# Attention with a feed-forward gate: part of the VectorE pair shifts given to GpSimd

## The chip, the cores and the metric

One core of a Trainium2 chip runs the program. It has five engines with a queue of instructions each: TensorE (PE in the profile, with its weight loads as PEld), ScalarE (ACT), VectorE (DVE), GpSimd (POOL) and SyncE (SP), which here issues DMAs. The metric is the time of one execution on the device, in microseconds (us).

## The reference

Multi-query attention over 2048 tokens with 32 heads of width 16, one K and one V for all heads, plus a gated feed-forward block on the same normalised input; the result is `x + attention * silu(ffn)`.

```python
xn = layernorm(x)                                   # 2048 x 512, bf16
q = (xn @ wq).reshape(B, S, 32, 16)                 # wq 512 x 512
k, v = xn @ wk, xn @ wv                             # 2048 x 16 each
p = softmax(einsum("bhqd,bkd->bhqk", q, k) * 16 ** -0.5)
s = einsum("bhqk,bkd->bhqd", p, v).reshape(B, S, 512) @ wo
f = (silu(xn @ w_gate) * (xn @ w_up)) @ w_down      # inner width 1792
out = x + s * silu(f)
```

## The kernel before

The scores of 32 heads x 2048 queries x 2048 keys are cut into 1024 tiles of 128 keys x 1024 columns (two heads x 512 queries). 32 blocks `b` (four chunks of 512 queries, four groups of eight heads, two halves) have 32 tiles each: 16 key tiles `t` for `x` = 0 and `x` = 1, the two pairs of heads of the block. Two matmuls of 32 rows each make a tile (`sc_emit`, L890) in one of three PSUM slots `ring[0..2]`. The tiles of `x` = 0 and `x` = 1 use different rows of the array, so the four matmuls of two tiles can run together.

A tile is exponentiated in one of two ways. Slots 0 and 1 belong to ScalarE: one exponential of 128x1024 from PSUM into one of `NPB` = 8 buffers `Pb` (`act_sc`, L950). Two such tiles, one of each `x`, are multiplied with `VA` in one group of four column-tiled matmuls (L760). Slot 2 belongs to VectorE (`dve_sc`): "passA" (L1004) turns the scores into 16-bit integers whose bits are a coarse power of two as fp16. Two passes, one of each `x`, fill one buffer `U` of 2048 columns; then for each of two constants `SHIFT[i]` an integer add of the whole buffer (the shift, `dS`, L1020) writes another buffer. The three buffers are multiplied with `VD[:, 0..2]`, which hold V times three coefficients, so that the sum of the three approximates the exponential: three groups of matmuls for a pair (L760). There are ten such buffers (six `Bf` and four quarters of `x_sb`).

All products of a block add up in the one PSUM bank `o_ps`, which VectorE copies out (`oev`, L773) before the next block's products. The sums of the softmax pass through small DMAs and a reciprocal, and GpSimd multiplies (`onorm`, L745). Beside this TensorE computes in the bank `m_ps` the q projections, the feed-forward block (gate and up, each evacuated by VectorE, L665 and L670; tanh on ScalarE, L666; product on GpSimd, L673; down projection, L686 and L688) and the output projection (L703, add on GpSimd, L708), each in groups of four column-tiled matmuls (`cmm`, L491).

No engine's order is left to the framework. A planner (`_Sched`) simulates the five engines at build time with a duration for each operation and a latency for each producer (`LAT`), and `chain` fixes each engine's order as planned. `pe_pick` chooses TensorE's next work: a score tile for ScalarE when a slot is free, other ready work if it ends within `TOL` of the time when that score could start, or, where TensorE would be idle for long enough, a group with zero weights (`zero`, `mzero`) if the recent activity is under `ACTMIN`. `pe_do` puts a VectorE tile into the same event as a ScalarE tile when slot 2 comes free within `MERGE`. Changing between score mode (row tiles) and the rest (column tiles) is planned at `SWITCH`. A block's last `D_LIM` = 12 tiles are not given to VectorE, which goes on with the next block. In the planner, shifts on VectorE and any operation on GpSimd exclude each other (`LOCKS`). The number of tiles that go to VectorE is not written anywhere: it comes out of this plan.

Of the kernel before, what the change touches and what calls it, by code (L numbers as in the profile page):

```python
# [14 lines left out]
ALU = mybir.AluOpType  # L15
# [13 lines left out]
SHIFT = (0.0, 683.0, 341.0)  # L29
# [3 lines left out]
NWARM, NJUNK = 13, 200  # L33
D_START, D_LIM, D_LIM_END = 26, 12, 8
F_ON, F_OFF = 26, 60
PB_URG, AHEAD, LAZY, ACTMIN, ACTLOW = 6, 16, 8, 9.0, 0.8
DPRI, DTOL, DWIN = -1.0, 0.12, 0.15
TOL, MERGE = 0.17, 0.25


def _dims(A_x, A_wq, B_w_gate):
# [143 lines left out]
class _Sched:  # L185
    LAT = {"PE": 0.205, "ACT": 0.22, "DVE": 0.25, "POOL": 0.16, "DMA": 0.0, "EXT": 0.0}
    SAME = {"PE": 0.0, "ACT": 0.0, "DVE": 0.1, "POOL": 0.05, "DMA": 0.0}
    SWITCH = 0.105
    HOT = 0.3
    LOCKS = ("dS", "xn")  # L190

# [94 lines left out]
def kernel(  # L286
# [13 lines left out]
    nc = tc.nc  # L300
# [37 lines left out]
                                        op0=ALU.mult, op1=ALU.add)  # L338
# [34 lines left out]
    xn = [sb([P, D], BF16, f"xn{i}") for i in range(4)]  # L373
    res = xn
    QB = [sb([P, 512], BF16, f"QB{i}") for i in range(2)]
    NPB = 8
    Pb = [sb([P, 1024], BF16, f"Pb{i}") for i in range(NPB)]
    XB = [g2_sb[:, 2 * i:2 * i + 2, :].rearrange("p n d -> p (n d)") for i in range(NT // 2)]
    Bf = [sb([P, 2048], U16, f"Bf{i}")[:] for i in range(6)]
# [117 lines left out]
    def OP(eng, dur, deps, emit, prio, mode=None, name=""):  # L497
        return sd.new(_Op(eng, dur, deps, emit, prio, mode, name))
# [3 lines left out]
        o.start = o.end = t  # L502
        return o

    MMF = 0.215
    NBLK = NSC * NQ * 2
    LN = 4 * (NSC - 1)
    NTILE = NBLK * NT * 2
# [144 lines left out]
    def hT_use(sc, f):  # L653
        return [hT_rd[0][1]] if hT_rd[0] is not None and hT_rd[0][0] == sc - 1 else []
    hT_last = [None]

    def g_ffn(sc, f):
        i = cnt["f"] % 2
        cnt["f"] += 1

        def mm(w, kc):
            return lambda: cmm(m_ps, w[:, kc, f * P:(f + 1) * P], xnT[:, kc, sc * 512:(sc + 1) * 512],
                               kc == 0, kc == KC - 1)
        a = grp_pe([mm(wg_sb, kc) for kc in range(KC)], [ffn_in])
        s_ = OP("DVE", 0.6, [a, ab_rel[i]], lambda: nc.vector.tensor_copy(out=ab[i][:], in_=m_ps[:]), (1,), name="gev")  # L665
        t_ = OP("ACT", 0.477, [s_, th_rel[i]], lambda: nc.scalar.activation(out=th[i][:], in_=ab[i][:], func=ACT.Tanh,  # L666
                                                                            scale=0.5), (0,), name="tanh")
        m_rel[:] = [s_]
        b = grp_pe([mm(wu_sb, kc) for kc in range(KC)], [ffn_in2])
        u_ = OP("DVE", 0.6, [t_, b], lambda: nc.vector.scalar_tensor_tensor(  # L670
            out=th[i][:], in0=th[i][:], scalar=1.0, in1=m_ps[:], op0=ALU.add, op1=ALU.mult), (1,), name="umul")
        m_rel[:] = [u_]
        h = OP("POOL", 1.25, [u_, s_] + hT_use(sc, f), lambda: nc.gpsimd.tensor_tensor(  # L673
            out=hT[:, f, :], in0=ab[i][:], in1=th[i][:], op=ALU.mult), (0,), name="hmul")
        ab_rel[i] = th_rel[i] = h
        h_done[f] = h
# [137 lines left out]
    def rem(b, x):  # L814
        r = NT - nx[b][x]
        if cur["pair"] is not None and cur["pair"][0] == b and cur["pair"][1] == 1 - x:
            r -= 1
        return r
# [162 lines left out]
    def get_buf():  # L981
# [9 lines left out]
        buf_rel[i] = [None]  # L991
        return i, rel

    def dve_sc(si, b, x, start, dur):
        sc, t = place_sc(si, b, x, start, dur)
        first = cur["pair"] is None
        u = cur["np"]
        if first:
            cur["ub"] = get_buf()
        ui, urel = cur["ub"]  # L1000
        U = Bf[ui]
        hs = slice(x * 1024, (x + 1) * 1024)
        pa = OP("DVE", 1.135, [sc] + urel,
                lambda: nc.vector.tensor_scalar(out=U[:, hs], in0=ring[si][:], scalar1=ubias,  # L1004
                                                scalar2=UINF, op0=ALU.add, op1=ALU.min), (1.5, u), name="passA")
        slot[si] = pa
        cur["pa"] = pa
        if first:
            cur["pair"] = (b, x, t, pa)
            return  # L1010
        _, x0, t0, pa0 = cur["pair"]
        cur["pair"] = None
        cur["np"] += 1
        pair_blk.append(b)
        half = b % 2
        tx = {x0: t0, x: t}
        terms, rd = [(ui, [pa, pa0], 0)], []
        for i in range(1, NPH):
            wi, wrel = get_buf()
            o = OP("DVE", 0.6, [pa, pa0] + wrel, lambda wi=wi, i=i: nc.vector.tensor_scalar(  # L1020
                out=Bf[wi], in0=U, scalar1=SHIFT[i], scalar2=None, op0=ALU.add), (2, u, i), name="dS")
            rd.append(o)
            terms.append((wi, [o], i))
        for bi, ops, vi in terms:
            mms = []
            dps = list(ops) + [oev[b - 1]]
            bufv = Bf[bi].bitcast(FP16)
            for g in range(4):
                tt = tx[g // 2]
                mms += mm_of(VD[:, vi], lambda g, bufv=bufv: bufv[:, g * 512:(g + 1) * 512], tt, half, (g,))  # L1030
                dps.append(v_ready[tt // 4][vi + 1])
            pv = OP("PE", MMF, dps, pv_emit(b, mms), (1, b, cur["nA"]), "c", "dpv")
            buf_rel[bi] = [pv] + (rd if vi == 0 else [])
            blk_pv[b].append(pv)
        check_done(b)
# [374 lines left out]
```

## Time and profile before

| | |
|---|---|
| median of 3 runs | 746.0 us (745.09 to 746.49) |
| the profiled execution | 744.99 us, its span from the first to the last instruction 743.1 us |
| TensorE busy | 721.5 us (97%), 8999 matmuls |
| ScalarE busy | 718.1 us (97%) |
| VectorE busy | 682.4 us (92%) |
| GpSimd busy | 127.0 us (17%) |
| granted TensorE clock, mean | 0.996 |
| DMA | 20.68 MB, mean 28 GB/s |

An engine's busy time counts instructions in flight; on ScalarE, VectorE and TensorE an instruction begins before the end of the one ahead of it, so the mean length of one is more than its share of the engine's time. The times of before that the working below rests on are those of the profiled execution.

### The profile page before, as it was taken

The numbers are of one execution on the slowest core, as the hardware profiler recorded it, in microseconds if no ns is written. First come the engines' busy times: TensorE is split into PE (matmuls) and PEld (weight loads), VectorE is DVE, ScalarE is ACT, GpSimd is POOL, SyncE is SP. The second block draws the span as 40 slices with busy tenths as digits, with TensorE's granted clock in tenths as the row PEclk, the third lists the DMA queues.
The fourth block names the chain that finished last, engine by engine and source line by source line (L and its number), as shares of the span: only waits on it lengthen the run. The fifth ranks groups of instructions, "written<-read, shape, count | busy, mean of one in ns | idle before, by whom it ended". The sixth has DMA issues, their size and how long they took to land.

```text
span 743.1 us, 20569 instructions
## 1 busy us (share of the span) xinstructions
PE 721.5 (97%) x8999; PEld 217.0 (29%) x8999; DVE 682.4 (92%) x886; ACT 718.1 (97%) x822; POOL 127.0 (17%) x120
## 2 busy tenths in 40 slices
PE   8999999999999999999999999999999999999994
PEld 3332222222222222222222322222222322322231
DVE  7779999999999899999999999999989999999995
ACT  5999999999999999999999999999999999999992
POOL 3212222200022222200013121220003222220001
PEclk9999999999999999999999999999999999999998
DMA  9400000000011100000001000000001000000001
GB/s 326 151 24 3 23 3 23 2 11 17 3 30 38 38 3 8 18 2 24 3 25 45 21 19 3 25 2 9 17 2 31 24 23 3 6 20 2 24 30 34
DMA packets 21722, 20.68 MB, mean 28 GB/s; under 512 B 8760, under 2 KB 17720, under 8 KB 21624
## 3 DMA queue, kind: packets, MB, share of 16 engines
q1 hardware_dynamic: 20040, 18.73, 8.3%
q8 instruction: 72, 1.18, 0.7%
q10 hardware_dynamic: 1584, 0.56, 0.3%
q14 instruction: 26, 0.21, 0.1%
HBM read 14.71 MB, written 2.34 MB: 23 GB/s over the span
## 4 chain that ended last, share of the span: by engine, by line
ACT 59%; PE 34%; DVE 4%; issue 2%; POOL 0%; ACTq 0%; DVEq 0%; POOLq 0%
ACT Pb L950 54%; PE ring L890 12%; PE o_ps L760 12%; PE m_ps L491 9%; ACT th L666 3%; ACT g_sb L950 1%; DVE Bf L1020 1%; DVE Bf L1004 1%; ACT th L686 1%; DVE x_sb L1020 1%; DVE x_sb L1004 1%; PE ring L491 0%; DVE ab L665 0%; PE ring L455 0%; DVE xn L708 0%
## 5 line engine op out<-in xcount | busy, mean ns | idle before, releaser
L950 ACT ACTIVATE Pb<-ring 128x1024 bf16<-128x1024 f32 x728 | 687.9, 1181 | 3.8 <-PE ring L890 1.9
L890 PE MATMUL ring<-QB,KT 32*128 32x512 bf16 x2048 | 291.7, 383 | 7.1 <-ACT Pb L950 3.9
L1004 DVE TENSOR_SCALAR Bf<-ring 128x1024 uint16<-128x1024 f32 x172 | 209.7, 1219 | 10.9 <-PE ring L890 9.2
L890 PEld LDWEIGHTS <-KT 32*128 32x128 bf16 x2048 | 84.9, 91 | 301.2 <-issue 297.1
L1004 DVE TENSOR_SCALAR x_sb<-ring 128x1024 uint16<-128x1024 f32 x116 | 141.5, 1220 | 7.6 <-PE ring L890 5.8
L760 PE MATMUL o_ps<-Pb,VA 128*32 128x512 bf16 x1456 | 140.5, 385 | 0.0
L673 POOL TENSOR_TENSOR hT<-ab,th 128x512 bf16<-128x512 f32 x56 | 78.2, 1396 | 356.7 <-DVE th L670 356.7
L760 PE MATMUL o_ps<-Bf,VD 128*32 128x512 f16 x1044 | 95.1, 384 | 1.2 <-DVE Bf L1020 1.1
L491 PE MATMUL m_ps<-wd_sb,hT 128*32 128x512 bf16 x896 | 72.5, 382 | 0.0
L491 PE MATMUL m_ps<-xnT,wg_sb 128*32 128x512 bf16 x896 | 72.3, 383 | 0.1
L1020 DVE TENSOR_SCALAR Bf<-Bf 128x2048 uint16<-128x2048 uint16 x101 | 72.1, 723 | 0.2
L491 PE MATMUL m_ps<-xnT,wu_sb 128*32 128x512 bf16 x896 | 68.4, 382 | 0.0
L760 PE MATMUL o_ps<-x_sb,VD 128*32 128x512 f16 x684 | 64.1, 384 | 0.0
L760 PEld LDWEIGHTS <-VD 128*32 128x32 f16 x1728 | 38.4, 94 | 60.1 <-issue 50.5
L760 PEld LDWEIGHTS <-VA 128*32 128x32 bf16 x1472 | 36.8, 94 | 54.2 <-issue 50.6
L1020 DVE TENSOR_SCALAR Bf<-x_sb 128x2048 uint16<-128x2048 uint16 x74 | 50.8, 694 | 0.3
L1020 DVE TENSOR_SCALAR x_sb<-Bf 128x2048 uint16<-128x2048 uint16 x71 | 50.5, 716 | 0.4
L745 POOL TENSOR_TENSOR oT<-oa,rb 128x512 bf16<-128x512 f32 x15 | 19.7, 1313 | 162.8 <-DMA rb<-dscr 153.0
L665 DVE COPY ab<-m_ps 128x512 f32<-128x512 f32 x56 | 38.3, 685 | 6.8 <-PE m_ps L491 6.4
L666 ACT ACTIVATE th<-ab 128x512 f32<-128x512 f32 x56 | 43.7, 781 | 0.0
L670 DVE SCALAR_TENSOR_TENSOR th<-th,m_ps 128x512 f32<-128x512 f32 x56 | 38.2, 682 | 4.0 <-PE m_ps L491 3.4
L1020 DVE TENSOR_SCALAR x_sb<-x_sb 128x2048 uint16<-128x2048 uint16 x42 | 29.5, 703 | 0.1
(115 smaller groups left out, 332.8 us busy)
## 6 DMA issues: line engine op xcount, KB each, us to landing
rb<-dscr SPq DMA_DIRECT2D x15, 256.0 KB
out_dram<-xn SPq DMA_DIRECT2D x16, 128.0 KB, 1.9
dn<-oa SPq DMA_DIRECT2D x120, 2.0 KB, 1.7
oa<-oa SPq DMA_DIRECT2D x60, 32.0 KB, 2.0
wg_sb<-in_B_w_gate_dram SPq DMA_DIRECT2D x1, 1792.0 KB, 11.6
wu_sb<-in_B_w_up_dram SPq DMA_DIRECT2D x1, 1792.0 KB
wd_sb<-in_B_w_down_dram SPq DMA_DIRECT2D x1, 1792.0 KB, 20.5
x_sb<-in_A_x_dram SPq DMA_DIRECT2D x3, 512.0 KB
```

The source lines that it names most:

```text
L491: return [nc.tensor.matmul(out=dst[GRP * j:GRP * j + GRP, :], lhsT=w[:, GRP * j:GRP * j + GRP], rhs=rhs, start=start, stop=stop, tile_posi ...
L665: s_ = OP("DVE", 0.6, [a, ab_rel[i]], lambda: nc.vector.tensor_copy(out=ab[i][:], in_=m_ps[:]), (1,), name="gev")
L666: t_ = OP("ACT", 0.477, [s_, th_rel[i]], lambda: nc.scalar.activation(out=th[i][:], in_=ab[i][:], func=ACT.Tanh, scale=0.5), (0,), name="t ...
L670: u_ = OP("DVE", 0.6, [t_, b], lambda: nc.vector.scalar_tensor_tensor(out=th[i][:], in0=th[i][:], scalar=1.0, in1=m_ps[:], op0=ALU.add, op ...
L673: h = OP("POOL", 1.25, [u_, s_] + hT_use(sc, f), lambda: nc.gpsimd.tensor_tensor(out=hT[:, f, :], in0=ab[i][:], in1=th[i][:], op=ALU.mult) ...
L686: t_ = OP("ACT", 0.477, [a, th_rel[i]], lambda: nc.scalar.activation(out=th[i][:, :D], in_=m_ps[:, :D], func=ACT.Tanh, scale=0.25), (0,), ...
L745: return [pk, q], lambda eng: eng.tensor_tensor(out=oT[qs % 2][:, jj, :], in0=o0[:], in1=rbt[:], op=ALU.mult)
L760: r.append(nc.tensor.matmul(out=o_ps[GRP * g:GRP * g + GRP, :], lhsT=lhs, rhs=rhs, start=(n == 0), stop=(n == pv_total[(b, g)] - 1), tile_ ...
L890: return lambda: [nc.tensor.matmul(out=ring[sl][:, u * 512:(u + 1) * 512], lhsT=KT[half][GRP * g:GRP * g + GRP, t * P:(t + 1) * P], rhs=QB ...
L950: bi = nc.scalar.activation(out=buf, in_=ring[i][:], func=ACT.Exp, scale=escale, bias=ebias)
L1004: lambda: nc.vector.tensor_scalar(out=U[:, hs], in0=ring[si][:], scalar1=ubias, scalar2=UINF, op0=ALU.add, op1=ALU.min), (1.5, u), name="p ...
L1020: o = OP("DVE", 0.6, [pa, pa0] + wrel, lambda wi=wi, i=i: nc.vector.tensor_scalar(out=Bf[wi], in0=U, scalar1=SHIFT[i], scalar2=None, op0=A ...
```

## The change

Of the integer shifts of a pair, some are given to GpSimd, as two instructions of 1024 columns each (a multiply by 1.0 and an add, on 16-bit integers); by the change's description three fifths of them. `pool_room` decides at planning: a shift goes to GpSimd if what GpSimd has ahead of it, counted from TensorE's planned time, is under `KB` = 2.5 us, and the block is not the current one with fewer than `KR` = 6 tiles left. The product of a shift then waits for both halves. Further: the zero-weight matmuls are planned only where the recent activity is under 0.6 (was 9.0); `TOL` goes from 0.17 to 0.21 and `MERGE` from 0.25 to 0.4; ScalarE's buffers `Pb` from 8 to 10, and with them the count of unfinished exponentials from which products are urgent (`PB_URG`) from 6 to 9; the planner's costs of a matmul group, a mode change and the feed-forward product are a little higher.

```diff
--- before.py
+++ after.py
@@ -33,9 +33,9 @@
 NWARM, NJUNK = 13, 200
 D_START, D_LIM, D_LIM_END = 26, 12, 8
 F_ON, F_OFF = 26, 60
-PB_URG, AHEAD, LAZY, ACTMIN, ACTLOW = 6, 16, 8, 9.0, 0.8
+PB_URG, AHEAD, LAZY, ACTMIN, ACTLOW = 9, 16, 8, 0.6, 0.8
 DPRI, DTOL, DWIN = -1.0, 0.12, 0.15
-TOL, MERGE = 0.17, 0.25
+TOL, MERGE, KB, KR, PSH = 0.21, 0.4, 2.5, 6, 1.12
 
 
 def _dims(A_x, A_wq, B_w_gate):
@@ -185,7 +185,7 @@
 class _Sched:
     LAT = {"PE": 0.205, "ACT": 0.22, "DVE": 0.25, "POOL": 0.16, "DMA": 0.0, "EXT": 0.0}
     SAME = {"PE": 0.0, "ACT": 0.0, "DVE": 0.1, "POOL": 0.05, "DMA": 0.0}
-    SWITCH = 0.105
+    SWITCH = 0.11
     HOT = 0.3
     LOCKS = ("dS", "xn")
 
@@ -373,7 +373,7 @@
     xn = [sb([P, D], BF16, f"xn{i}") for i in range(4)]
     res = xn
     QB = [sb([P, 512], BF16, f"QB{i}") for i in range(2)]
-    NPB = 8
+    NPB = 10
     Pb = [sb([P, 1024], BF16, f"Pb{i}") for i in range(NPB)]
     XB = [g2_sb[:, 2 * i:2 * i + 2, :].rearrange("p n d -> p (n d)") for i in range(NT // 2)]
     Bf = [sb([P, 2048], U16, f"Bf{i}")[:] for i in range(6)]
@@ -502,7 +502,7 @@
         o.start = o.end = t
         return o
 
-    MMF = 0.215
+    MMF = 0.216
     NBLK = NSC * NQ * 2
     LN = 4 * (NSC - 1)
     NTILE = NBLK * NT * 2
@@ -670,7 +670,7 @@
         u_ = OP("DVE", 0.6, [t_, b], lambda: nc.vector.scalar_tensor_tensor(
             out=th[i][:], in0=th[i][:], scalar=1.0, in1=m_ps[:], op0=ALU.add, op1=ALU.mult), (1,), name="umul")
         m_rel[:] = [u_]
-        h = OP("POOL", 1.25, [u_, s_] + hT_use(sc, f), lambda: nc.gpsimd.tensor_tensor(
+        h = OP("POOL", 1.3, [u_, s_] + hT_use(sc, f), lambda: nc.gpsimd.tensor_tensor(
             out=hT[:, f, :], in0=ab[i][:], in1=th[i][:], op=ALU.mult), (0,), name="hmul")
         ab_rel[i] = th_rel[i] = h
         h_done[f] = h
@@ -991,6 +991,12 @@
         buf_rel[i] = [None]
         return i, rel
 
+    p_ops = []
+
+    def pool_room(b):
+        late = b <= cur["ba"] and rem(b, 0) + rem(b, 1) < KR
+        return not late and max(sd.free["POOL"] - sd.free["PE"], 0.0) + sum(o.dur for o in p_ops if o.start is None) < KB
+
     def dve_sc(si, b, x, start, dur):
         sc, t = place_sc(si, b, x, start, dur)
         first = cur["pair"] is None
@@ -1017,10 +1023,18 @@
         terms, rd = [(ui, [pa, pa0], 0)], []
         for i in range(1, NPH):
             wi, wrel = get_buf()
-            o = OP("DVE", 0.6, [pa, pa0] + wrel, lambda wi=wi, i=i: nc.vector.tensor_scalar(
-                out=Bf[wi], in0=U, scalar1=SHIFT[i], scalar2=None, op0=ALU.add), (2, u, i), name="dS")
-            rd.append(o)
-            terms.append((wi, [o], i))
+            if pool_room(b):
+                def shift(z, wi=wi, i=i):
+                    return lambda: nc.gpsimd.tensor_scalar(out=Bf[wi][:, z], in0=U[:, z], scalar1=1.0,
+                                                           scalar2=SHIFT[i], op0=ALU.mult, op1=ALU.add)
+                o = [OP("POOL", PSH, [pa, pa0] + wrel, shift(slice(h * 1024, h * 1024 + 1024)), (1, u, i), name="pS")
+                     for h in range(2)]
+                p_ops.extend(o)
+            else:
+                o = [OP("DVE", 0.6, [pa, pa0] + wrel, lambda wi=wi, i=i: nc.vector.tensor_scalar(
+                    out=Bf[wi], in0=U, scalar1=SHIFT[i], scalar2=None, op0=ALU.add), (2, u, i), name="dS")]
+            rd += o
+            terms.append((wi, o, i))
         for bi, ops, vi in terms:
             mms = []
             dps = list(ops) + [oev[b - 1]]
```

## Rows read from the trace of the kernel before

**Rows 1.** The page, busy time of each engine and the clock in 40 slices.

```profile
PE 721.5 (97%) x8999; PEld 217.0 (29%) x8999; DVE 682.4 (92%) x886; ACT 718.1 (97%) x822; POOL 127.0 (17%) x120
...
PEclk9999999999999999999999999999999999999998
```

**Rows 2.** Timeline of ScalarE, 300 to 312: start, length, engine, line, operation, count.

```profile
299.46 7.51 ACT L950 ACTIVATE Pb<-ring 128x1024 bf16<-128x1024 f32 x8
306.70 0.78 ACT L666 ACTIVATE th<-ab 128x512 f32<-128x512 f32 x1
307.22 5.76 ACT L950 ACTIVATE Pb<-ring 128x1024 bf16<-128x1024 f32 x6
```

**Rows 3.** Groups by line and shape, whole span: count, busy us, mean ns.

```profile
L950 ACT ACTIVATE Pb<-ring 128x1024 bf16<-128x1024 f32 x728 | 687.9, 1181 | 3.8 <-PE ring L890 1.9 <-PE o_ps L760 1.8
...
L666 ACT ACTIVATE th<-ab 128x512 f32<-128x512 f32 x56 | 43.7, 781 | 0.0
...
L760 PE MATMUL o_ps<-xnT,zw 128*32 128x512 bf16 x336 | 27.6, 383 | 0.0
```

**Rows 4.** The chain that ended last, in order of time: start, length, piece.

```profile
481.60 5.50 ACT Pb L950 x6
```

**Rows 5.** Waits, whole span: total us, times, longest.

```profile
ACT Pb L950 <- PE ring L890: 1.9, 4, 0.8
...
PE o_ps L760 <- DVE Bf L1020: 1.1, 4, 0.4
```

**Rows 6.** Busy time by line, whole span: TensorE's products (L760), projections and feed-forward (L491).

```profile
0.00:743.10 743.10, 288.85 (x3536) 72.56 (x3536) 1.00 0.09 28
...
0.00:743.10 743.10, 255.81 (x3232) 66.29 (x3232) 1.00 0.09 28
```

**Rows 7.** Timeline of TensorE: score events of both tile kinds, and what lies between.

```profile
12.44 0.40 PE L890 MATMUL ring<-QB,KT 32*128 32x512 bf16 x4
...
318.29 0.39 PE L890 MATMUL ring<-QB,KT 32*128 32x512 bf16 x4
318.61 0.61 PE L491 MATMUL m_ps<-wd_sb,hT 128*32 128x512 bf16 x8
319.16 0.39 PE L890 MATMUL ring<-QB,KT 32*128 32x512 bf16 x2
...
720.02 0.39 PE L890 MATMUL ring<-QB,KT 32*128 32x512 bf16 x4
```

**Rows 8.** Busy time by line, whole span: VectorE's passes (L1004) and shifts (L1020).

```profile
0.00:743.10 743.10, 351.18 (x288) 1.00 0.09 28
...
0.00:743.10 743.10, 200.25 (x288) 1.00 0.09 28
```

**Rows 9.** Timeline of VectorE: the first pass, four in the middle, the last.

```profile
43.16 1.22 DVE L1004 TENSOR_SCALAR Bf<-ring 128x1024 uint16<-128x1024 f32 x1
...
316.00 1.22 DVE L1004 TENSOR_SCALAR x_sb<-ring 128x1024 uint16<-128x1024 f32 x1
317.14 0.91 DVE L1020 TENSOR_SCALAR Bf<-Bf 128x2048 uint16<-128x2048 uint16 x1
...
720.88 1.22 DVE L1004 TENSOR_SCALAR Bf<-ring 128x1024 uint16<-128x1024 f32 x1
```

**Rows 10.** Groups by line and shape: GpSimd with one input and with two.

```profile
L708 POOL TENSOR_TENSOR xn<-ab,xn 128x512 bf16<-128x512 f32 x12 | 14.7, 1222 | 27.0 <-DVE ab L703 27.0
...
L487 POOL TENSOR_SCALAR VD<-vf 128x128 f16<-128x128 f32 x12 | 3.5, 301 | 0.6
...
L428 POOL COPY hT<-wk_sb 128x512 bf16<-128x512 bf16 x1 | 0.6, 611 | 2.5 <-DMA wk_sb<-in_A_wk_dram 2.5
```

**Rows 11.** Timeline of GpSimd around 316.

```profile
316.23 1.27 POOL L673 TENSOR_TENSOR hT<-ab,th 128x512 bf16<-128x512 f32 x1 [5.69 <-DVE th L670]
```

## The prediction

> **What bounds the kernel now.** I read the page's busy shares first [rows 1]: TensorE and ScalarE both show 97%, VectorE 92%, GpSimd 17%. Two engines at 97% need a second look, because a busy TensorE is not a full one.
>
> ScalarE is really full. In steady work eight exponentials and the start of the tanh behind them are 7.24 us apart (299.46 to 306.70) [rows 2], so one exponential costs 0.905 to 0.917 us of ScalarE, though its own row says 1181 ns [rows 3]: neighbours overlap. I take 0.917, the pace of the chain where nothing interrupts it (six in 5.50 us [rows 4]). 736 of the 1024 score tiles go this way (728 in the row shown and 8 into another buffer), or 675 us; 72 tanh (the 56 of the row shown [rows 3] and 16 of the down steps) of 0.52 us each (306.70 to 307.22 [rows 2]) add 37; the rest of the 743.1 us span is the start and the tail. ScalarE's largest wait for a score matmul sums to 1.9 us [rows 5]. So in the middle there is nothing else to gain: **the span moves by 0.917 us for each tile that leaves ScalarE**, as long as the others keep up.
>
> TensorE is less full than it looks. Its rows [rows 6] give (3536 + 3232) / 4 = 1692 column groups of four matmuls, 84 of them with zero weights (336 matmuls [rows 3]), which only fill idle time. Two groups and the change back to score mode take 0.55 us (318.61 to 319.16) and a score event with its change 0.32 (318.29 to 318.61) [rows 7]: 0.215 a group, about 0.11 a change, so 0.43 us an event. A row of four score matmuls in 0.39 or 0.40 us is a ScalarE tile and a VectorE tile in one event, for the price of one; the timeline has 268 such rows, of which the first and the last are shown [rows 7]. Some 756 events x 0.43 + 1608 useful groups x 0.215 = 325 + 346 = 671 us, against 708 us between those two rows alone (12.44 to 720.02). At least 37 us are free.
>
> VectorE takes the other 288 tiles: one pass from PSUM each (1.22 us by its row, 351.18 / 288, and 1.14 from its start to the next instruction, 316.00 to 317.14), and two shifts a pair, 288 in all (about 0.70 us by row, 0.6 in pace) [rows 8, 9]. The first pass starts at 43.16 and the last at 720.88 [rows 9]: 287 intervals in 677.7 us, 2.36 us each. **This interval sets how many tiles VectorE can take off ScalarE.** Sorting the 287 by how many other VectorE instructions lie between two passes: none, 1.75 us (8 intervals); one, 1.93 (137); two, 2.56 (91); three, 3.11 (42). The first instruction between two passes is nearly free, since the next pass must wait anyhow for PSUM slot 2 to be refilled; the second costs 0.6. On average there are 1.69: one shift, and 0.69 of other work (the 201 evacuations and feed-forward steps of that stretch).
>
> **The change, part by part.** *Shifts to GpSimd.* By its description three fifths of the shifts move, so 0.4 shifts stay per tile. With about 315 tiles the other work is 201 / 315 = 0.64, together 1.04 per interval. Spread as a quarter with none, half with one, a fifth with two and a few with three: 0.25 x 1.75 + 0.5 x 1.93 + 0.21 x 2.56 + 0.04 x 3.11 = **2.06 us**. The stretch that holds VectorE's tiles is the span less 65.4 us (743.1 - 677.7), and each tile more shortens the span by 0.917: N x 2.06 = 677.7 - 0.917 x (N - 288), so N = 942 / 2.98 = 316. That is 28 tiles, 14 pairs, more than now, and 28 x 0.917 = **25.7 us** less.
>
> *The price on GpSimd.* A moved shift is two instructions of 1024 columns; the trace of before has none. The nearest rows are a one-input copy of 512 16-bit columns in 611 ns and a one-input multiply-add of 128 columns in 301 [rows 10]; the line through them is 0.81 ns a column, and 1.03 us at 1024. The other end is the two-input multiply of 512 columns in 1222 ns [rows 10], twice that for 1024 columns: 2.44 us. I take 1.1, since a shift has one 16-bit input; the plan in the diff assumes 1.12. Then 158 pairs x 1.2 shifts x 2 = 379 halves x 1.1 = 417 us, beside some 110 us of GpSimd's present 127 [rows 1]. That fits the 652 us that are left of the stretch. The GpSimd products that queue behind the shifts (the feed-forward product, the normalisation, the residual add) come one or two in 10 us and have two buffers; a delay of 2 to 4 us is covered by that, and without the cover would hold up the m_ps bank.
> The Trainium skill (GPSIMD Engine Reference, Engine selection) advises against GpSimd for elementwise work, as about half as fast with two inputs, and calls one-input work roughly line-rate; by its first half the upper end would hold and the change would lose, by its second the lower; the rows above lean to the second.
>
> *TensorE.* 14 pairs moved add 28 groups (three groups a pair where ScalarE's tiles took one), 6 us, and save 28 events x 0.43 = 12. It then needs about 665 of 682 us: 17 free instead of 37, less what it waits in joint events (MERGE 0.25 to 0.4 and TOL 0.17 to 0.21: at most 0.15 us more each, on a few tens of events, 0 to 6 us). With so little slack I charge ScalarE **3 us** of new waits (0 to 10).
>
> *Zero matmuls.* Removing nearly all of 84 x 0.215 = 18 us costs and gains nothing by itself, for they fill idle time. The granted clock is full in every slice but the last, where the work has ended [rows 1]; the useful work rises, so I expect it to stay. If a slower slice came, events and groups in it would double; 10 us of that would cost up to 10 us.
>
> *Ten exponential buffers, the other threshold for urgent products, the new planner costs:* no instruction more. They let ScalarE run ahead where products wait; the waits they could remove sum to a few us [rows 5], so 0 to 2 us. No DMA is added, and SP's queue keeps its order of issue.
>
> Sum: 743.1 - 25.7 + 3 = 720.4 us of span. The profiled execution took 744.99, 1.9 more than its span, and the median of the runs is 1.0 above that: 720.4 + 2.9, about 723. The buffers may give back 0 to 2, so I say **722 us**.
>
> **The rivals.** *The lock eats the gain.* In the trace VectorE's shift and GpSimd exclude each other: the GpSimd product that starts at 316.23 ends at 317.50 [rows 11], and the shift issued at 317.14 takes 0.91 us [rows 9] instead of the mean 0.70, as if it began at its end. The Trainium skill (SBUF, Who interferes with whom) states an exclusive lock between GpSimd and VectorE's two-port modes for the whole instruction; this row agrees with it. Today GpSimd is busy 17% of the time; with 417 + 110 us it would be 80%. If the 126 shifts left on VectorE met it at random, 0.8 x 0.55 us each, 55 us or 0.17 a tile, the interval would be 2.23, N 299, and the time 722 + 16 = **738**. Against it: the planner already keeps these instructions apart.
> *GpSimd becomes the bound*, the case on the other side. 379 halves of d us, 110 of other work and 76 of excluded shifts (126 x 0.6) must fit the stretch. At d = 1.30 they fill the present 677.7 us and the whole gain is gone; with 1.4, which still lies between the two ends, they need 717, and the time is 717 + 65 + 3 = **785**. TensorE takes its instructions in order, so a late product of a shift holds up the next score, and through it ScalarE; today its largest wait for a shift sums to 1.1 us [rows 5]. For it: no row shows this operation. Against it: both one-input rows.
> *The plan does not place more tiles.* TensorE's quantum is coarse: per exponential it fits an event and 2.3 groups (0.917 - 0.43 over 0.215), and 1636 / 708 = 2.3 are asked for. If it has no room for more tiles, shifts move and the count stays near 290: **743**, within a few us of now.
> *More than forecast.* If nearly each interval is 1.93, N = 942 / 2.85 = 331, and the time 722 - 14 = **708**, if TensorE has the room.
>
> **How the numbers follow.** Forecast (712 to 730) 0.47; lock 0.18; more 0.08; no more tiles 0.11; GpSimd bound, or another stall that costs all, 0.16. The likeliest gives 722. The range goes from 705, below the case of more tiles (708), to 747, past the case without more tiles; what lies outside is mostly the slower one. A measurement here can tell 0.2%, 1.5 us, from no change. Faster by more than that: 0.47 + 0.18 + 0.08 + half of 0.11 = 0.78; within it 0.06; slower 0.16.
>
> **What would show it.** Right: some 708 tiles on ScalarE and 316 on VectorE, ScalarE still at 97%, passes 2.06 us apart, half shifts of 1.0 to 1.1 us on GpSimd and their sum near 420. Lock: VectorE shifts of 0.9 us and more in their mean. GpSimd bound: half shifts over 1.3, and TensorE waiting for GpSimd's buffer. Full TensorE: ScalarE waiting over 10 us for scores, tile counts as now. The forecast is wrong at its root if the number of tiles moved and the fall of the span do not stand at 0.917 us a tile.

## The result, and the profile after

The changed kernel takes 753.9 us in the median (749.9 to 766.7, 7 runs), the kernel before 745.6 on the same chip: **slower, ratio 1.0094 (95% interval 1.0074 to 1.0114)**, or 7.0 us. The run of 766.7 us fell into a slower state of the chip (granted clock 0.965); it is in the median but not in the ratio, and all ratios below, each to the kernel before on the same chip, leave such runs out. Differences between runs are taken from these ratios, as parts of 745.6 us. The forecast was 722 us, in a range of 705 to 747.

The page after, against [rows 1]: VectorE lost 67 us of work and GpSimd won 386. TensorE's and ScalarE's busy times fell by only 5.6 and 3.5 us, while the span grew by 10.5. In the clock's row the last two slices are under 9, where before only the last one was.

```profile
span 753.6 us, 20505 instructions
PE 715.9 (95%) x8748; PEld 210.9 (28%) x8748; DVE 615.6 (82%) x730; ACT 714.6 (95%) x812; POOL 513.0 (68%) x472
...
PEclk9999999999999999999999999999999999999988
```

Groups by line and shape, against [rows 3], then busy time by line over the whole span, against [rows 8]: ScalarE's exponentials, one row of four of GpSimd's half shifts and two of four of VectorE's shifts; then VectorE's passes, GpSimd's half shifts and VectorE's shifts in sum (a window that ends behind the span covers all of it).

```profile
L950 ACT ACTIVATE Pb<-ring 128x1024 bf16<-128x1024 f32 x718 | 677.7, 1091 | 15.5 <-PE ring L890 13.7
...
L1028 POOL TENSOR_SCALAR Bf<-Bf 128x1024 uint16<-128x1024 uint16 x124 | 138.2, 1125 | 37.6 <-DVE Bf L1010 30.1 <-PE ring L890 2.4 <-PE o_ps L760 1.5
...
L1034 DVE TENSOR_SCALAR Bf<-Bf 128x2048 uint16<-128x2048 uint16 x50 | 47.1, 949 | 0.6
...
L1034 DVE TENSOR_SCALAR x_sb<-Bf 128x2048 uint16<-128x2048 uint16 x30 | 24.3, 813 | 0.1
```
```profile
0.00:753.60 753.60, 363.24 (x298) 0.99 0.09 27
...
0.00:753.60 753.60, 394.02 (x352) 0.99 0.09 27
...
0.00:775.00 775.00, 107.15 (x122) 0.99 0.09 27
```

ScalarE has 726 tiles (718 and 8 into the other buffer) and VectorE 298: **ten tiles moved, not 28**. 352 half shifts, 176 of 298 shifts, went to GpSimd at 394.02 / 352 = 1.12 us. The 122 shifts left on VectorE take 0.88 us each instead of 0.70.

Waits over the whole span, VectorE's first, before and then after, and then, against [rows 5], ScalarE's and TensorE's after:

```profile
DVE Bf L1004 <- PE ring L890: 9.2, 26, 0.8
DVE ab L665 <- PE m_ps L491: 6.4, 19, 1.2
DVE x_sb L1004 <- PE ring L890: 5.8, 15, 0.8
DVE th L670 <- PE m_ps L491: 3.4, 13, 0.4
...
DVE Bf L1010 <- PE ring L890: 38.8, 73, 1.4
DVE x_sb L1010 <- PE ring L890: 20.8, 37, 1.7
DVE ab L665 <- PE m_ps L491: 14.5, 22, 1.7
DVE th L670 <- PE m_ps L491: 9.8, 17, 1.1
...
ACT Pb L950 <- PE ring L890: 13.7, 26, 1.5
...
PE m_ps L491 <- DVE ab L665: 3.8, 4, 1.3
PE ring L890 <- DVE Bf L1010: 3.3, 5, 1.0
PE o_ps L760 <- DVE Bf L1034: 2.3, 6, 0.8
```

ScalarE waits 13.7 us for scores (1.9 before), and VectorE 59.6 us for its own scores (9.2 + 5.8 before) and 24.3 us for the groups in `m_ps` that it evacuates at L665 and L670 (9.8 before). How such a wait comes about can be read in the timeline around 617, engine by engine: two of VectorE's shifts beside two of GpSimd's products, then TensorE, then ScalarE, and the stretch from 620 to 625 with TensorE's busy time, its matmuls and the granted clock (0.66).

```profile
617.08 3.48 DVE L1034 TENSOR_SCALAR Bf<-Bf 128x2048 uint16<-128x2048 uint16 x2
620.48 0.68 DVE L645 TENSOR_SCALAR QB<-m_ps 128x512 bf16<-128x512 f32 x1
```
```profile
617.06 1.27 POOL L745 TENSOR_TENSOR oT<-oa,rb 128x512 bf16<-128x512 f32 x1 [0.21 <-DMA rb<-dscr]
618.29 1.72 POOL L673 TENSOR_TENSOR hT<-ab,th 128x512 bf16<-128x512 f32 x1
```
```profile
621.21 0.62 PE L491 MATMUL m_ps<-xnT,wg_sb 128*32 128x512 bf16 x4 [1.01 <-DVE QB L645]
```
```profile
622.41 1.02 ACT L950 ACTIVATE Pb<-ring 128x1024 bf16<-128x1024 f32 x1 [1.47 <-PE ring L890]
```
```profile
620.00:625.00 5.00, 3.99 (x32) 0.66 0.00 0
```

Two shifts that need 1.3 us take 3.48. The first waits for GpSimd's product that began 0.02 us earlier; then GpSimd's next product takes 1.72 instead of 1.27, since it waits for that shift; and the second shift ends 0.55 us after this product's end at 620.01. The evacuation behind them is 2 us late, TensorE, whose order is fixed, waits 1.01 us for it, ScalarE 1.47 us for the score behind that, and TensorE's clock falls to its lower level (1.2 GHz) for a part of the stretch.

### The profile page after: what moved, and what is told of

It is laid out like the page before. It is cut to its first block, busy times and chain, and to the rows that moved or that the text cites. A ratio compares the mean times of both kernels' runs of the same rounds, so it can differ in the third digit from the quotient of the medians.

```text
span 753.6 us, 20505 instructions
## 1 busy us (share of the span) xinstructions
PE 715.9 (95%) x8748; PEld 210.9 (28%) x8748; DVE 615.6 (82%) x730; ACT 714.6 (95%) x812; POOL 513.0 (68%) x472
## 4 chain that ended last, share of the span: by engine, by line
PE 53%; ACT 26%; DVE 11%; issue 3%; DMA 3%; SPq 2%; POOL 2%; DVEq 0%; POOLq 0%; ACTq 0%
ACT Pb L950 23%; PE ring L890 19%; PE o_ps L760 17%; PE m_ps L491 15%; DVE x_sb L1010 3%; DVE Bf L1034 2%; SPq L787 2%; DVE Bf L1010 2%; DMA dn<-oa 2%; ACT th L666 1%; DVE x_sb L1034 1%; ACT g_sb L950 1%; DVE ab L665 1%; PE ring L436 1%; DVE oa L773 1%
## 5 line engine op out<-in xcount | busy, mean ns | idle before, releaser
L950 ACT ACTIVATE Pb<-ring 128x1024 bf16<-128x1024 f32 x718 | 677.7, 1091 | 15.5 <-PE ring L890 13.7
L890 PE MATMUL ring<-QB,KT 32*128 32x512 bf16 x2048 | 300.6, 386 | 13.9 <-ACT Pb L950 7.6
L1010 DVE TENSOR_SCALAR Bf<-ring 128x1024 uint16<-128x1024 f32 x190 | 231.6, 1219 | 41.8 <-PE ring L890 38.8
L1028 POOL TENSOR_SCALAR Bf<-Bf 128x1024 uint16<-128x1024 uint16 x124 | 138.2, 1125 | 37.6 <-DVE Bf L1010 30.1
L1010 DVE TENSOR_SCALAR x_sb<-ring 128x1024 uint16<-128x1024 f32 x108 | 131.6, 1219 | 21.9 <-PE ring L890 20.8
L760 PE MATMUL o_ps<-Pb,VA 128*32 128x512 bf16 x1436 | 133.8, 386 | 0.0
L1028 POOL TENSOR_SCALAR x_sb<-Bf 128x1024 uint16<-128x1024 uint16 x96 | 108.7, 1141 | 29.8 <-DVE Bf L1010 17.7
L760 PE MATMUL o_ps<-Bf,VD 128*32 128x512 f16 x1080 | 97.9, 387 | 4.6 <-DVE Bf L1034 2.3
L1028 POOL TENSOR_SCALAR Bf<-x_sb 128x1024 uint16<-128x1024 uint16 x70 | 77.2, 1110 | 23.5 <-DVE x_sb L1010 16.2
L1028 POOL TENSOR_SCALAR x_sb<-x_sb 128x1024 uint16<-128x1024 uint16 x62 | 70.6, 1146 | 22.0 <-DVE x_sb L1010 12.1
L491 PE MATMUL m_ps<-xnT,wg_sb 128*32 128x512 bf16 x896 | 75.6, 386 | 1.2 <-DVE QB L645 1.0
L491 PE MATMUL m_ps<-xnT,wu_sb 128*32 128x512 bf16 x896 | 71.4, 385 | 3.8 <-DVE ab L665 3.8
L491 PE MATMUL m_ps<-wd_sb,hT 128*32 128x512 bf16 x896 | 71.7, 383 | 0.0
L760 PE MATMUL o_ps<-x_sb,VD 128*32 128x512 f16 x708 | 66.5, 388 | 0.2 <-DVE x_sb L1034 0.2
L760 PEld LDWEIGHTS <-VD 128*32 128x32 f16 x1788 | 40.8, 95 | 59.4 <-issue 47.6
L665 DVE COPY ab<-m_ps 128x512 f32<-128x512 f32 x56 | 38.4, 685 | 15.8 <-PE m_ps L491 14.5
L760 PEld LDWEIGHTS <-VA 128*32 128x32 bf16 x1452 | 34.5, 94 | 55.8 <-issue 52.0
L670 DVE SCALAR_TENSOR_TENSOR th<-th,m_ps 128x512 f32<-128x512 f32 x56 | 38.2, 682 | 12.9 <-PE m_ps L491 9.8
L1034 DVE TENSOR_SCALAR Bf<-Bf 128x2048 uint16<-128x2048 uint16 x50 | 47.1, 949 | 0.6
```

The source lines that it names most:

```text
L491: return [nc.tensor.matmul(out=dst[GRP * j:GRP * j + GRP, :], lhsT=w[:, GRP * j:GRP * j + GRP], rhs=rhs, start=start, stop=stop, tile_posi ...
L760: r.append(nc.tensor.matmul(out=o_ps[GRP * g:GRP * g + GRP, :], lhsT=lhs, rhs=rhs, start=(n == 0), stop=(n == pv_total[(b, g)] - 1), tile_ ...
L890: return lambda: [nc.tensor.matmul(out=ring[sl][:, u * 512:(u + 1) * 512], lhsT=KT[half][GRP * g:GRP * g + GRP, t * P:(t + 1) * P], rhs=QB ...
L950: bi = nc.scalar.activation(out=buf, in_=ring[i][:], func=ACT.Exp, scale=escale, bias=ebias)
L1028: return lambda: nc.gpsimd.tensor_scalar(out=Bf[wi][:, z], in0=U[:, z], scalar1=1.0, scalar2=SHIFT[i], op0=ALU.mult, op1=ALU.add)
L1034: o = [OP("DVE", 0.6, [pa, pa0] + wrel, lambda wi=wi, i=i: nc.vector.tensor_scalar(out=Bf[wi], in0=U, scalar1=SHIFT[i], scalar2=None, op0= ...
```

## The experiments

Three theories: **A**, GpSimd and the shifts left on VectorE meet at the port they share (the prediction's name for what makes them exclude each other), VectorE falls behind the fixed order and TensorE and ScalarE wait; **B**, without zero groups the clock falls; **C**, the other parts of the change (thresholds, buffers) cost the time.

**Half shifts of 32 columns, then VectorE's shifts of 64 columns, then both.** Same order, waits and counts as in the changed kernel; part of the shifts is left out.

```diff
+            wd = 32 if wi in full else 1024
...
-                o = [OP("POOL", PSH, [pa, pa0] + wrel, shift(slice(h * 1024, h * 1024 + 1024)), (1, u, i), name="pS")
+                o = [OP("POOL", PSH, [pa, pa0] + wrel, shift(slice(h * 1024, h * 1024 + wd)), (1, u, i), name="pS")
...
-                    out=Bf[wi], in0=U, scalar1=SHIFT[i], scalar2=None, op0=ALU.add), (2, u, i), name="dS")]
+                    out=Bf[wi][:, 0:2 * wd], in0=U[:, 0:2 * wd], scalar1=SHIFT[i], scalar2=None, op0=ALU.add), (2, u, i), name="dS")]
```

> The changed kernel with the same order, waits and instruction counts on every engine, but each GpSimd half shift covers 32 columns instead of 1024 (full width only the first time a buffer is written), so part of the shift is left out and GpSimd hardly holds the port it shares with VectorE. Theory A (the port: GpSimd and the 122 shifts left on VectorE meet, VectorE falls behind its order, TensorE and then ScalarE wait): VectorE shifts back to 0.70 us mean, the granted clock back to 0.99 or more, and the time about 736 us (745.6 less 10 tiles x 0.917), 733 to 740. Theory B (the clock: with few zero-weight groups left TensorE's clock falls at each stall): 748 or more, clock near 0.987. Theory C (the order itself is worse: longer waits for joint events): 748 or more with VectorE shifts at 0.70.

> The changed kernel with the same order and waits, but the 122 shifts left on VectorE cover 64 columns instead of 2048 (part of the shift left out); GpSimd does its 352 half shifts at full width. Theory A (the port): nearly no meeting is left, GpSimd halves at 1.05 us, time 735 to 742. A variant of it, that GpSimd's halves are simply too long for the order, expects the time to stay at 748 or more. Theories B and C: 748 or more.

> The changed kernel with the same order, waits and counts, and both kinds of shift cut down (32 columns on GpSimd, 64 on VectorE, full width only the first time a buffer is written; part of the shifts left out). It shows what the order alone is worth with neither the port nor the shifts' time in it. If the port accounts for the loss, it is no faster than the kernel with thin VectorE shifts alone: 735 to 739. If VectorE's and GpSimd's own time matter beside the port, it is several us faster: 728 to 734.

Measured: thin GpSimd 743.8 us (ratio 0.9951, 0.9930 to 0.9972); thin VectorE 738.2 (0.9869, 0.9840 to 0.9897); both 737.0 (0.9874, 0.9847 to 0.9901). VectorE's shifts in sum in the first, and ScalarE's wait in the second:

```profile
0.00:775.00 775.00, 90.20 (x122) 0.99 0.09 27
```
```profile
ACT Pb L950 <- PE ring L890: 5.0, 9, 1.0
```

With the 122 VectorE shifts cut down hardly anything is left that could meet, and 1.31% is gained over the kernel before: 0.0131 x 745.6 = 9.8 us, which is about the ten tiles (10 x 0.917 = 9.2). Cutting down GpSimd's half shifts as well brings nothing more, so **GpSimd's own time costs nothing that can be measured; VectorE's shifts beside GpSimd's do cost**: 1.0094 - 0.9869, or 16.8 us, together with those shifts' own time. With only GpSimd cut down the VectorE shifts keep their width and are at 0.74 us, and 10.7 of these us are gone (1.0094 - 0.9951). That much is the meeting. The other 6.1 us are not divided among the shifts' own time, their meetings with GpSimd's other products, and the clock, which was 0.988 to 0.995 in these runs and 0.990 to 0.994 in those with thin VectorE shifts. A's number for this run, 736, was too low. B expected 748 or more in the first two, so few zero groups are not the main cause. C is refuted for the order: it is worth its ten tiles.

**The other parts alone, and the shifts alone.** The first is the changed kernel with `pool_room` always refusing; the second the kernel before with `pool_room` and the half shifts added and every other number left.

> All parts of the change but the shifts to GpSimd: thresholds, ten buffers, few zero-weight groups, new planner costs, and all shifts on VectorE. The program has 292 VectorE tiles, against 288 before and 298 with the change. Theory A (the port): VectorE shifts at 0.70 us, granted clock 0.995, time 741 to 746 (4 tiles x 0.917 under before at best). Theory C (the other parts cost the time): 750 or more. Theory B (few zero groups let the clock fall): clock under 0.99 and 748 or more. On the tile count: if VectorE's work set it, 292 with twice and a half the shifts on VectorE could not stand beside 298; if the pace of the joint events sets it, the mean interval of the passes is 2.3 us in both.

> The kernel before with the shifts to GpSimd alone: old thresholds, eight buffers, old zero groups and planner costs. 290 VectorE tiles, 350 half shifts on GpSimd, 115 shifts on VectorE. Theory A (the port): VectorE shifts 0.82 us and more, ScalarE waiting over 10 us for scores, time 752 to 768. Theory C: 743 to 748, as before the change.

Measured: 747.0 us (ratio 1.0005, 0.9989 to 1.0022) and 774.4 us (1.0391, 1.0373 to 1.0409). VectorE's shifts in sum, in the first and the second, and ScalarE's wait in each:

```profile
0.00:775.00 775.00, 206.65 (x292) 0.99 0.09 27
...
0.00:790.00 790.00, 98.04 (x115) 0.99 0.09 26
```
```profile
ACT Pb L950 <- PE ring L890: 7.2, 19, 0.5
...
ACT Pb L950 <- PE ring L890: 14.3, 21, 1.8
```

The other parts change nothing that can be measured, although four tiles (3.7 us) leave ScalarE: it waits 7.2 us for scores there instead of 1.9, and the granted clock is 0.989 instead of the 0.995 that A expected. The shifts cost, at 0.71 us a VectorE shift in the first and 0.85 in the second. C falls as the cause of the loss. The shifts alone cost 29 us, more than A expected, and the whole change 7, so beside the other parts the shifts cost less; by which of them is not shown. Of the 29, more than half lies behind the last pass (732.6 to the span's end at 771.6, 39 us where the kernel before needs 22), and I have not followed that tail.

**The order of the port made binding.** Semaphores hold each VectorE shift behind the GpSimd instruction planned ahead of it, and the reverse.

```diff
+        if o.eng == "POOL" or o.eng == "DVE" and o.name in sd.LOCKS:
+            other = port.get("DVE" if o.eng == "POOL" else "POOL")
+            if other is not None and pending.get(o.eng):
+                tc.add_manual_dep(r.ins, other.ins.name, _sync, reason="port")
...
```

> The changed kernel with the planned order of the shared port made binding: semaphores let a VectorE shift start only when the GpSimd instruction planned ahead of it has ended, and the other way round. If the loss comes from GpSimd overtaking (a VectorE shift that waits for several GpSimd instructions in a row), the VectorE shifts fall to 0.70 to 0.75 us and the time to 738 to 746. If meeting at the port costs the same whoever goes first, or the semaphores cost more than the meeting, 750 to 760.

Measured: 748.9 us (1.0032, 1.0021 to 1.0044). A row of VectorE's shifts, and what GpSimd now waits for:

```profile
L1034 DVE TENSOR_SCALAR Bf<-Bf 128x2048 uint16<-128x2048 uint16 x50 | 34.1, 688 | 10.6 <-POOL Bf L1028 4.3 <-POOL x_sb L1028 3.0 <-POOL hT L673 2.6
```
```profile
POOL x_sb L1028 <- DVE Bf L1034: 38.6, 22, 3.5
POOL Bf L1028 <- DVE Bf L1034: 27.2, 19, 3.0
POOL Bf L1028 <- DVE x_sb L1034: 21.5, 16, 2.5
```

The shifts are at 0.69 us, so nothing meets any more, and 4.6 of the 7.0 us of loss are gone. But against the thin VectorE shifts (0.9869) 12.2 us remain: VectorE's shifts now wait 20.7 us in all for GpSimd's instructions and GpSimd 116 us for those shifts, which points to taking turns in the planned order as most of what the meeting cost. What the semaphores themselves take of it is not shown. The time lies between the two expectations.

**More shifts to GpSimd, and shorter holds.** `KB` 9.0 for 2.5; and each half shift as two instructions of 512 columns.

```diff
-TOL, MERGE, KB, KR, PSH = 0.21, 0.4, 2.5, 6, 1.12
+TOL, MERGE, KB, KR, PSH = 0.21, 0.4, 9.0, 6, 1.12
```
```diff
+                    return lambda: [nc.gpsimd.tensor_scalar(out=Bf[wi][:, c:c + 512], in0=U[:, c:c + 512], scalar1=1.0,
+                                                            scalar2=SHIFT[i], op0=ALU.mult, op1=ALU.add)
+                                    for c in range(z.start, z.stop, 512)]
```

> The changed kernel with GpSimd's allowed backlog at 9 us instead of 2.5: 472 half shifts on GpSimd (four fifths of the shifts), 58 left on VectorE, 294 VectorE tiles. Theory A in the form that the loss lies in VectorE shifts that wait for the port: half as many shifts can wait, so their excess over 0.70 us falls to about half of the changed kernel's and the time to 742 to 750. In the form that GpSimd is late by itself (its halves delayed, products waiting for them): GpSimd busy over 600 us, time 755 to 775, and TensorE waits for GpSimd's buffers. By the interval formula of the prediction 0.2 shifts a tile should have given over 320 tiles; 294 speaks for the pace of the joint events.

> The changed kernel with the same plan, but each GpSimd half shift issued as two instructions of 512 columns. A VectorE shift that meets GpSimd can take the port after a piece of about half the length. If the length of one hold of the port is what makes VectorE late, the excess of the VectorE shifts over 0.70 us falls to about half and the time by 3 to 6 us, to 748 to 751. If the VectorE shift has to wait for all that GpSimd has ready, or the added instructions (352 more, each with its fixed cost) make GpSimd late, the excess stays and the time is 754 to 765.

Measured: 770.5 us (1.0300, 1.0239 to 1.0361) and 749.2 us (1.0037, 1.0023 to 1.0050). VectorE's shifts in sum, in the first and in the second, then the second's pieces on GpSimd:

```profile
0.00:790.00 790.00, 59.44 (x58) 0.98 0.09 26
...
0.00:775.00 775.00, 105.16 (x122) 0.98 0.09 27
...
0.00:775.00 775.00, 459.50 (x704) 0.98 0.09 27
```

With four fifths on GpSimd each VectorE shift waits longer (1.02 us), the sum of the excess stays near 19 us, GpSimd is busy 81% of the span (621 us), and TensorE waits 9.7 us for its buffers: the first form of A was wrong here and the second right. Shorter holds gave 4.2 us, within the 3 to 6 that A expected. How, the trace cannot show: the profiled execution took 753.9 us, as long as the changed kernel, and in it the excess of the shifts, 0.86 - 0.70, is nearly that of the changed kernel, 0.88 - 0.70.

**The zero groups.** The old threshold (`ACTMIN` 9.0), which also changes the plan; then 20 zero groups put into the changed kernel's own plan where it leaves TensorE idle, 29 into that of the other parts alone, and 20 into the ordered kernel.

```diff
+        if pe_end is not None and at is not None and left[at] and o.start - pe_end >= 0.3:
+            fills[id(o)] = pv_emit(at, [(zw[:], xnT[:, 0, 0:512], g) for g in range(4)])
...
```

> The changed kernel with the old threshold for zero-weight groups (9.0 for 0.6); the plan comes out a little different, with 732 exponentials instead of 726. Theory B (clock): granted clock 0.995 as before the change, time 743 to 748. Theory A (port): the clock recovers but VectorE shifts stay at 0.85 us and above, and the time at 749 to 756.

> The changed kernel with its plan untouched, and 20 zero-weight groups put into TensorE's order where the plan leaves it idle for 0.3 us or more between two products of one block. Theory B' (the missing zero groups cost clock, on top of the port): the granted clock rises from 0.987 to about 0.993 and the time falls by 3 to 6 us, to 748 to 751. If the clock falls only behind stalls that no plan foresees, it stays near 0.987 and the time at 752 to 756.

> The kernel with all parts of the change but the shifts to GpSimd (746 us, clock 0.989), its plan untouched, and 29 zero-weight groups put where the plan leaves TensorE idle for 0.3 us or more between two products of one block. Theory B': clock 0.994 and 742 us, which is 745.8 less 4 tiles x 0.917. If not: clock 0.989 and 745 to 748.

> The changed kernel with the binding order of the shared port and the 20 zero-weight groups. Theory B': 3 to 5 us under the 748.9 of the ordered kernel, 744 to 746, which would be level with the kernel before: what is then left of the loss is the waiting for the port in planned order. If not: 748 to 750.

Measured: 768.0 us (1.0288, 1.0260 to 1.0317), clock 0.988; 752.8 us (1.0094, 1.0078 to 1.0110), clock 0.990 in the profiled run and 0.994 to 0.995 in the other three; 745.0 us (0.9998, 0.9981 to 1.0015), clock 0.996 in the profiled run and 0.982 to 0.996 in the others; 757.2 us (1.0151, 1.0114 to 1.0188), clock 0.986. In the second of these the only stretch at the lower clock that is left in the steady part lies at its end:

```profile
720.00:725.00 5.00, 5.00 (x36) 0.50 0.00 0
```

So filler in the planned gaps does bring the clock up in most runs of the second and third kernel, but no time that can be measured: the ratio is 1.0094 with and without it in the changed kernel, and 0.9998 against 1.0005 in the other parts, where B' expected the four tiles' 3.7 us. The missing zero groups alone are not the loss: with the clock back the changed kernel is as slow as it was. The old threshold makes another plan, slower by 14 us, whose clock falls all the same. That the ordered kernel became 9 us slower with the same 20 groups nobody expected, and it stays open.

**A longer wait for joint events.** `MERGE` 0.9 for 0.4.

> The changed kernel with MERGE at 0.9 instead of 0.4: a ScalarE score event waits up to 0.9 us for VectorE's slot, so that VectorE's next tile is in it. The program has 308 VectorE tiles. If the refill of slot 2, which is tied to ScalarE's events, is what holds the interval of the passes, VectorE's waits for scores fall from 60 us to under 40, the intervals with one evacuation from 2.25 to about 2.0 and the mean from 2.33 to 2.2, with as many shifts on VectorE as before. If VectorE's own work or the port holds it, the intervals stay. The time itself is not expected to gain: what TensorE waits in joint events is taken from the feed-forward work, which ends later; 755 to 800 us.

Measured: 818.3 us (1.0966, 1.0836 to 1.1095; two runs), above the 755 to 800 expected: the last pass starts at 746.2, and 74 us of work are left behind it, where the changed kernel has 21. The 307 intervals between VectorE's passes (41.19 to 746.22) have a mean of 2.30 us; those with one evacuation and no shift between the passes take 2.04 us (90), with nothing 1.78 (110). TensorE's score rows and what they wait for:

```profile
L890 PE MATMUL ring<-QB,KT 32*128 32x512 bf16 x2048 | 328.3, 389 | 31.5 <-DVE Bf L1010 15.5 <-DVE x_sb L1010 8.7 <-ACT Pb L950 3.5
```

The short intervals shrink as expected, with more shifts on VectorE than before this edit. In those with one evacuation VectorE's mean wait ahead of the pass falls from 0.13 to 0.05 us and ahead of the evacuation from 0.31 to 0.22, so the wait for the refill is part of them: some 0.09 of the 0.21 us that these intervals lost, and waiting ahead of the evacuation as much again. But VectorE's waits for scores stay at 67 us and the mean hardly moves: TensorE now waits 24 us for VectorE's slot, and the long intervals are longer.

## Why the prediction was wrong

**ScalarE bounds, at 0.917 us a tile: borne out where the others keep up.** Ten tiles moved and the two kernels without meetings are 9.4 and 9.8 us faster. In the other parts alone the condition fails: four tiles moved, nothing was gained, and ScalarE waits 7.2 us for scores.

**The interval of the passes: the step that failed first.** The counts held: the forecast had a quarter of the intervals with nothing between the passes, half with one instruction, a fifth with two, a few with more, and the trace of the changed kernel (297 intervals from 41.10 to 732.33) has 72, 151, 51 and 23. With the lengths of the kernel before these counts give 2.10 us; the trace has 2.33.

```profile
41.10 1.23 DVE L1010 TENSOR_SCALAR Bf<-ring 128x1024 uint16<-128x1024 f32 x1 [0.35 <-PE ring L890]
...
732.33 1.23 DVE L1010 TENSOR_SCALAR Bf<-ring 128x1024 uint16<-128x1024 f32 x1
```

The lengths did not hold. I took them from the kernel before by count alone, and most of its single instructions were shifts, which are ready whenever VectorE is (it waits 0.01 us ahead of one in the mean). From the timelines of VectorE, mean us (number of intervals):

| between two passes | before | after | thin VectorE shifts | other parts alone |
|---|---|---|---|---|
| nothing | 1.75 (8) | 1.85 (72) | 1.85 (72) | 1.75 (11) |
| one shift | 1.92 (92) | 1.93 (51) | 1.86 (51) | 1.86 (98) |
| one other instruction | 1.94 (45) | 2.25 (100) | 2.29 (100) | 1.94 (49) |
| a shift and another | 2.56 (72) | 2.79 (26) | 2.69 (26) | 2.57 (63) |

Taking the shift out of an interval saves 0.07 us when it was alone there. Where it stood beside an evacuation it should have saved 0.6 and saved 0.3: VectorE, free earlier, waits for TensorE instead. The timelines show for what. Of the 0.31 us by which the interval with one other instruction grew, 0.22 are waiting ahead of that instruction (0.09 before, 0.31 after), mostly for TensorE's group in `m_ps`, and 0.09 waiting ahead of the pass (0.04, then 0.13), for the refill of slot 2. The prediction knew the second wait only. The third column shows that neither the port nor the shifts' time does this. Why TensorE's groups come later there is not settled.

How many tiles VectorE gets is fixed by the plan, before the chip runs: 292 with every shift on VectorE, 298 with three fifths moved, 294 with four fifths, 308 with the longer joint wait. So 18 of the 28 tiles were never there: 18 x 0.917 = **16.5 us**. The meetings come on top: the mean interval is 2.27 us with thin VectorE shifts, 2.33 with full ones, 2.06 in the forecast. In the plan too the shifts and GpSimd exclude each other (`LOCKS`); no run takes that out, so its part in the count is not shown.

**GpSimd's price: right.** 1.1 us was taken for a half shift, 1.12 was measured, and 394 us in sum (352 halves) instead of 417 (379). It did not become the bound.

**The port: a rival whose price is near by luck.** It was given 16 us: 55 us of waiting, spread over the intervals, make 299 tiles of 316, and 17 tiles are 16 us. Measured are 10.7 to 16.8 us with the count of tiles unchanged, so the mechanism behind the price was another. The VectorE shifts are only 0.18 x 122 = 22 us longer, but their lateness reaches TensorE's fixed order. ScalarE's waits for scores, charged with 3 us more, grow by 3.1 with thin VectorE shifts (5.0 against 1.9) and by 11.8 with full ones. The argument against this rival, that the planner keeps the two apart, is what the timeline at 617 refutes: the plan's order of two engines is no order on the chip unless a semaphore makes it one. Made one, it gave back 4.6 us.

**Exclusive rivals: the second failure.** "Lock" and "no more tiles" stood as alternatives to the forecast and to one another, and both were priced in tiles that do not move. In the runs the missing tiles and the meeting are two things, and both came: 722 + 16.5 + 16.8 = 755.3, and 753.9 was measured (752.6 by the ratio). None of the priced cases had a meeting that stalls TensorE and ScalarE at an unchanged count of tiles; only "another stall that costs all", which has no price, has room for it. The two prices as they stood, added up, would have counted the same tiles twice. The reason given for few tiles, TensorE's quantum, is not shown either.

**The clock: wrong.** "I expect it to stay" failed (0.996 to 0.987 in the profiled executions). Of the three stretches ahead of the tail in which it fell, two lie behind stalls in which TensorE waits for VectorE, 1.32 us at 271 and 1.01 us at 620. The third and longest begins at 720, behind a stretch in which TensorE is busy for 3.98 of 5 us with no gap over 0.53 us. The other parts alone, with VectorE's shifts at 0.71 us, lose the clock behind a like stretch at 712, and with filler in it they keep it in the profiled execution; the kernel before has other work at that time and is busy for all of the 5 us. So few zero groups, which the prediction set at nothing, can cost clock where the plan leaves TensorE idle. First the stall at 271, then TensorE's busy time and clock after, before, in the other parts alone, and in these with filler:

```profile
272.25 0.61 PE L491 MATMUL m_ps<-xnT,wu_sb 128*32 128x512 bf16 x8 [1.32 <-DVE ab L665]
```
```profile
715.00:720.00 5.00, 3.98 (x44) 1.00 0.00 2
720.00:725.00 5.00, 4.66 (x28) 0.51 0.00 0
...
715.00:720.00 5.00, 5.00 (x66) 1.00 0.01 3
...
705.00:710.00 5.00, 3.80 (x42) 1.00 0.00 0
...
715.00:720.00 5.00, 5.00 (x38) 0.50 0.01 3
...
705.00:710.00 5.00, 4.10 (x48) 1.00 0.00 0
...
715.00:720.00 5.00, 5.00 (x64) 1.00 0.01 3
```

Two of the changed kernel's runs had a clock of 0.992 and took 749.9 and 750.3 us; four had 0.987 or 0.988 and took 753.5 to 755.4. So some 4 us go with the clock from run to run, as its effect or beside it; filler, which brings the clock back, did not bring them back.

**The other parts at 0 to 2 us: right in size** (1.0005), though what stands in it is not what was forecast: four tiles' 3.7 us less, 5.3 us more waiting for scores, and a lower clock.

None of the kernels that compute everything beats the kernel before; the best, the other parts with filler, is level with it.

## What to carry to other kernels

How long an interval is, sorted by how much stands in it, is valid only for the same things standing in it: before work is taken off an engine, look at what it will wait for next, and count the waits that have no room to shrink. Moving part of an operation to an engine that excludes what stays behind makes what stays behind longer and late, here 122 shifts from 0.70 to 0.88 us; keeping all of it where it was avoids the meeting, moving four fifths was worse, and moving all was not tried. And rivals are alternatives only where one mechanism rules out the other: write down which wait each of them lengthens, and add those that can come together.

## What the runs showed of the hardware

VectorE's 16-bit shifts and GpSimd's instructions exclude each other, and where both engines had work ready, at 617, they took turns, one instruction each. The longest of the 122 VectorE shifts takes 1.80 us, no more than its own 0.68 and one product of 1.27; the longest of GpSimd's 352 half shifts takes 1.58, against 1.04 alone. So neither was seen waiting for several instructions of the other in a row.

A 16-bit multiply-add on GpSimd takes, in the median, 1.044 us for 1024 columns, 0.621 for 512 and 0.216 for 32. These three lie on one line, 0.83 ns a column on a fixed 0.19 us; the prediction's line through other rows had 0.81 ns.

TensorE's clock was granted at its lower level behind stalls of 1.32 us (at 271) and 1.01 us (at 620) in the changed kernel, but not behind others as long (1.13 us at 119 and 1.03 us at 419 had no fall behind them), and also behind a stretch whose gaps are at most 0.53 us.

The longest shift and half shift of the changed kernel (minimum, median and maximum in ns), then GpSimd's half shifts in the ordered kernel, with pieces of 512 columns, and of 32:

```profile
L1034 DVE TENSOR_SCALAR Bf<-Bf x50: 677/694/1801, 53.7 to 734.8; 128x2048 uint16<-128x2048 uint16 x50
...
L1028 POOL TENSOR_SCALAR x_sb<-Bf x96: 1039/1045/1582, 65.8 to 732.7; 128x1024 uint16<-128x1024 uint16 x96
...
L1028 POOL TENSOR_SCALAR x_sb<-Bf x96: 1039/1044/1049, 71.1 to 732.5; 128x1024 uint16<-128x1024 uint16 x96
...
L1028 POOL TENSOR_SCALAR x_sb<-Bf x192: 613/621/1147, 66.7 to 731.9; 128x512 uint16<-128x512 uint16 x192
...
L1033 POOL TENSOR_SCALAR x_sb<-Bf x96: 209/216/717, 65.6 to 718.4; 128x32 uint16<-128x32 uint16 x96
```
